# Split-weight attention with a maxout feed-forward: the lower parts of a chunk's weights made in its own period

## The chip, the cores and the metric

The kernel runs on one core of one Trainium2 chip. The metric is the device time of one execution in microseconds, as a median of several. A profile of one execution shows, for each engine, every instruction with its start, its length and the source line that issued it. The engines are TensorE (PE in the profile; its weight loads PEld), VectorE (DVE), ScalarE (ACT), GpSimd (POOL) and SyncE, whose queue of transfers is SP.

## The reference

Attention with normalized queries and keys runs on 8 batches of 12 heads, 448 rows of 64 numbers each. Its output, 3584 rows of 768, goes through a feed-forward layer with three input matrices, whose products are combined by their maximum, and one output matrix.

```python
def rmsnorm(x, g):
    rms = np.sqrt(np.mean(x * x, axis=-1, keepdims=True) + 1e-06)
    return x / rms * g
q_n, k_n = (rmsnorm(q, g_q), rmsnorm(k, g_k))
scores = scale * np.matmul(q_n, k_n.transpose(0, 1, 3, 2))
scores = scores - np.max(scores, axis=-1, keepdims=True)
attn = np.exp(scores)
attn = attn / (np.sum(attn, axis=-1, keepdims=True) + 1e-09)
attn_out = np.matmul(attn, v)
...
h = np.maximum(np.maximum(x @ w1, x @ w2), x @ w3)
return h @ w_out
```

## The kernel before

**Tiling.** A *group* `g` is a pair of heads of one batch; there are 48, six to a batch. A group is worked in four *chunks* `c` of 112 query rows, both heads side by side. `k = 4 * g + c` counts the chunks through. The first six groups (`PLAIN`) are computed in float32. From group 6 on, each float32 operand of a product is split into two float16 numbers, an upper and a lower part, and a product is the sum of three (`TERMS`: upper by upper, upper by lower, lower by upper).

**One split chunk.** `scores` (L553) puts six products into a PSUM buffer `sc`, of which there are two. `row_max` (L562, VectorE) takes the largest score of each row. `softmax` scales it (L570, ScalarE, into `nm`) and writes the exponentials of both heads over the scores in `sc` (L579, ScalarE, twice), with their sums beside them. `upper_weights` turns the sums into `rs` (L648 and L652, VectorE) and writes the upper parts of the normalized weights to `pp` (L655, ScalarE, once for each head). `lower_weights` writes the lower parts, `sc * rs` minus the upper part (L665, VectorE, once for each head); with them `sc` is read for the last time, and scores of a later chunk may go into that buffer. `turn_weights` (L675) is a DMA transpose of `pp` (three buffers) into `pt`, issued on SP. `add_values` (L703) multiplies a whole group's `pt` by the split values, and `finish` splits the result (L717 on ScalarE, then L718 on VectorE) for the feed-forward.

**The order.** All five engines run in exactly the order in which the code issues the work; each takes its own instructions from a queue and waits at the head of it. The order is made by `beat(g, i)`, called twelve times for a group. `c, part = divmod(i, 3)`: a chunk's *period* is three beats. In part 0 VectorE gets the chunk's row maximum and then the lower parts of the chunk before, and ScalarE the softmax; in part 1 come `upper_weights`; in part 2 the scores of the next chunk. Each beat also issues a piece of the feed-forward of an earlier batch on TensorE (`thirds`, L732 and L796, some two of its units a beat), and, through `later`, what these products need on VectorE and ScalarE one or more beats after (L742, L746, L752, L756, L805). Other beats square and sum the rows of a later group (`squares`, L372), split them (`upper_rows`, L434; `lower_rows`, L440), turn them on SP (`turn_rows`, L450), split the values (L525, L531), load later groups (L330, L342, L346, L347), and decode the feed-forward's weights (L188 to L205, L268 to L275, L307 to L315) during the first eleven or so groups.

In the beat, `w = g - 1` is the group whose weights are complete. Its fourth chunk is transposed at `i == 2`, the first three chunks of the group at hand at `i` = 5, 8 and 11. `add_values(w)` stands at `i == 7`.

Of the kernel before, what the change touches and what calls it, by code (L numbers as in the profile page):

```python
# [35 lines left out]
PLAIN = 6  # L36
# [3 lines left out]
def qknorm_attention_maxout_ffn_kernel(  # L40
# [48 lines left out]
    G = B * NP  # L89
# [448 lines left out]
    def scores(g, c):  # L538
        s = st[g]
        sc = ps_s.tile([P, 2, 512], F32, name="sc", tag="s")  # L540
        s["sc", c] = sc
        if g < PLAIN:
            qt = s["qs"].rearrange("p (c r) -> p c r", c=NQ)
            for h, rows in enumerate(HALVES):
                nc.tensor.matmul(
                    sc[:QP, h, :S], qt[rows, c], s["ks"][rows, KEYS[h]],
                    start=True, stop=True,
                )
            return
        qt, kt = s["qs"], s["ks"].rearrange("p a c r -> p a (c r)")  # L550
        for n, (qp, kp) in enumerate(TERMS):
            for h, rows in enumerate(HALVES):
                nc.tensor.matmul(  # L553
                    sc[:QP, h, :S], qt[rows, qp, c], kt[rows, kp, KEYS[h]],
                    start=n == 0, stop=n == len(TERMS) - 1,
                )
# [3 lines left out]
    def row_max(g, c):  # L560
        sc = st[g]["sc", c]
        nc.vector.tensor_reduce(  # L562
            sc[:QP, 0, S + 8:S + 10], sc[:QP, :, :S], axis=AX, op=ALU.max, negate=True
        )

    def softmax(g, c):
        s = st[g]
        sc = s["sc", c]
        nm = sb.tile([QP, 2], F32, name="nm", bufs=3)
        nc.scalar.activation(nm, sc[:QP, 0, S + 8:S + 10], AF.Copy, scale=down[:QP])  # L570
        if g < PLAIN:
            if c == 0:
                s["sum"] = sb.tile([QP, NQ, 2], F32, name="sum", bufs=2)
            s["e", c] = sb.tile([QP, 2, S], F32, name="e", tag="pp", bufs=3)
        for h in range(2):
            to, total = sc[:QP, h, :S], sc[:QP, 1, S + 8 + h:S + 9 + h]
            if g < PLAIN:
                to, total = s["e", c][:, h], s["sum"][:, c, h:h + 1]
            nc.scalar.activation(  # L579
                to, sc[:QP, h, :S], AF.Exp, bias=nm[:, h:h + 1], scale=down[:QP],  # L580
                accum_out=total,
            )
# [7 lines left out]
    def turn_plain(g, c):  # L590
        s = st[g]
        e = s.pop(("e", c)).rearrange("p h k -> p (h k)")
        if c == 0:
            s["pt"] = sb.tile([P, 14, S], F16, name="pt", bufs=2)
        s["turned"] = []
        sc = s.pop(("sc", c))
        for i, (u0, n) in enumerate(((0, 4), (4, 3))):
            turned = sc[:, i]
            if g < PLAIN:
                turned = ps_m.tile([P, 512], F32, name="turned", tag="m")  # L600
            for u in range(n):
                nc.tensor.transpose(
                    turned[:, u * QP:(u + 1) * QP],
                    e[:, (u0 + u) * P:(u0 + u + 1) * P], ident[:QP, :QP],
                )
            s["turned"].append((u0, n, turned))

    def keep_turned(g, c):
        s = st[g]
        for u0, n, turned in s.pop("turned"):  # L610
            nc.scalar.copy(
                pt_plain(s)[:, u0:u0 + n, c * QP:(c + 1) * QP],
                turned[:, :n * QP].rearrange("p (u q) -> p u q", u=n),
            )


    def guard_sums(g):
        rs = st[g]["sum"]
        nc.scalar.activation(rs, rs, AF.Copy, bias=SUM_EPS)

    def inverse_sums(g):
        rs = st[g]["sum"]
        nc.vector.reciprocal(rs, rs)
# [14 lines left out]
    def keep_sums(g):  # L638
        s = st[g]
        s["by"] = sb.tile([P, S], F32, name="by", tag="m", bufs=2)  # L640
        nc.scalar.copy(s["by"], s.pop("spread")[:, :S])
# [19 lines left out]
    def lower_weights(g, c):  # L661
        s = st[g]
        sc, rs, pp = s.pop(("sc", c)), s.pop(("rs", c)), s["pp", c]
        for h in range(2):
            nc.vector.scalar_tensor_tensor(  # L665
                out=pp[:, 1, h], in0=sc[:QP, h, :S], scalar=rs[:, h:h + 1],
                in1=pp[:, 0, h], op0=ALU.mult, op1=ALU.subtract,
            )
# [39 lines left out]
    def scale_plain(g):  # L708
        s = st[g]
        av = s["av"][:, :S]  # L710
        nc.vector.tensor_tensor(out=av, in0=av, in1=s.pop("by"), op=ALU.mult)
# [209 lines left out]

    def beat(g, i):
        w, n = g - 1, g + 2
        c, part = divmod(i, 3)
        k = 4 * g + c
        early = k + 1 <= 4 * PLAIN
        if part == 0:  # L930
            if g < G:
                if k > 4 * PLAIN:
                    row_max(g, c)
                softmax(g, c)
            if early:
                scores(*divmod(k + 1, 4))
            if 0 < k <= 4 * PLAIN:
                turn_plain(*divmod(k - 1, 4))
            elif 0 < k <= 4 * G:
                lower_weights(*divmod(k - 1, 4))  # L940
        if part == 1:
            if 0 < k <= 4 * PLAIN:
                keep_turned(*divmod(k - 1, 4))
            if PLAIN <= g < G:
                upper_weights(g, c)
        if part == 2:
            if early:
                row_max(*divmod(k + 1, 4))
            elif k + 1 < 4 * G:
                scores(*divmod(k + 1, 4))  # L950
        if 0 <= w < PLAIN:
            if i == 1:
                guard_sums(w)
            if i == 2:
                inverse_sums(w)
            if i == 5:
                spread_sums(w)
            if i == 6:
                keep_sums(w)
            if i == (8 if w < PLAIN else 9):  # L960
                scale_plain(w)
        if w >= 0 and i == (4 if w < PLAIN else 7):
            add_values(w)
        thirds(THIRDS[i] + (len(queue) > 1 and i % 6 == 4))
        if w >= 0 and i == (9 if w < PLAIN else 10):
            finish(w, x_of[w // NP])
        if w >= 0 and g % NP == 0 and i == (6 if w < PLAIN else 10):
            queue.append(ffn(w // NP, x_of[w // NP]))

        if g + 1 < G:  # L970
            if g + 1 < PLAIN:
                if i in (1, 4):
                    turn_whole(g + 1, "kq"[i // 4])
                if i in (2, 5):
                    keep_whole(g + 1, "kq"[i // 5])
            else:
                if i in (0, 1):
                    upper_rows(g + 1, "kq"[i])
                if i in (2, 3):
                    lower_rows(g + 1, "kq"[i - 2])  # L980
                if i in (4, 5):
                    turn_rows(g + 1, "kq"[i - 4])

        if n < G:
            if i in (0, 3):
                squares(n, "kq"[i // 3])
            if i in (2, 5):
                sum_squares(n, "kq"[i // 3])
            if i in (5, 7):
                inv_rms(n, "kq"[i // 7])  # L990
            if i == 8:
                scale_k(n)
            if i == 9:
                scale_q(n)

        if g == 0 and i < 7:
            load_v(i)
            later(3, lambda: largest_v(i))
        if 0 < g < G - 6 and i == 5:
            load_v(g + 6)  # L1000
            later(4, lambda: largest_v(g + 6))
        if g == 0 and i == 9:
            bound_v(0)
        if g > 1 and g % NP == 0 and g < G and i == 1:
            bound_v(g // NP)
        if PLAIN <= g < G and i == 9:
            scale_v(g)
        if PLAIN <= g < G and i == 11:
            upper_v(g)
        if PLAIN <= w and i == 0:  # L1010
            lower_v(w)

        if g + 3 < G:
            if i == 0:
                load_k(g + 3)
            if i == 1:
                load_q(g + 3)
        if i == 2 and w >= PLAIN:
            turn_weights(w, 3)
        if PLAIN <= g < G and i in (5, 8, 11):  # L1020
            turn_weights(g, i // 3 - 1)
        n_in = min(decoded[0], NFT * NJ)
        due_at = BLOCK_BEATS[0] * n_in + BLOCK_BEATS[1] * (decoded[0] - n_in)
        if decoded[0] < len(blocks) and clock[0] > due_at:
            later(0, lambda n=decoded[0]: prep_block(n), True)
            decoded[0] += 1
        tick()
# [41 lines left out]
```

## Time and profile before

| | before |
|---|---|
| median of 3 runs | 1101.73 us (1098.24 to 1102.97) |
| the profiled execution | 1103.44 us, its span 1101.6 us |
| PE busy | 1018.6 us (92%) |
| DVE busy | 757.8 us (69%) |
| ACT busy | 772.1 us (70%) |
| POOL busy | 702.4 us (64%) |
| mean granted PE clock | 0.957 |

The span is the time from the first to the last instruction of the profiled execution. A group's row gives the line, engine and operation, what it writes and reads, its count, then busy time and the mean length of one, then the idle time of its engine just before it and what ended that. A row of waits tells who waited for whom, for how long in total, how often, and the longest. In rows in order of time, two or more instructions of one kind that follow each other are one row, with their count behind an x.

### The profile page before, as it was taken

The numbers are of one execution on the slowest core, as the hardware profiler recorded it, in microseconds if no ns is written. First come the engines' busy times: TensorE is split into PE (matmuls) and PEld (weight loads), VectorE is DVE, ScalarE is ACT, GpSimd is POOL, SyncE is SP. The second block draws the span as 40 slices with busy tenths as digits, with TensorE's granted clock in tenths as the row PEclk, the third lists the DMA queues.
The fourth block names the chain that finished last, engine by engine and source line by source line (L and its number), as shares of the span: only waits on it lengthen the run. The fifth ranks groups of instructions, "written<-read, shape, count | busy, mean of one in ns | idle before, by whom it ended". The sixth has DMA issues, their size and how long they took to land. (4 is left out here: it accounts for less than half of the span.)

```text
span 1101.6 us, 18390 instructions
## 1 busy us (share of the span) xinstructions
PE 1018.6 (92%) x6168; PEld 501.9 (46%) x6168; DVE 757.8 (69%) x1390; ACT 772.1 (70%) x1767; POOL 702.4 (64%) x805
## 2 busy tenths in 40 slices
PE   4678768988999999999999999999999999999998
PEld 2334333434444455444544454444444454445555
DVE  3899988888667676677677776777677766762210
ACT  4599887767868678687877777778777787773001
POOL 5477988856767767678677686776867677610000
PEclk9687868998989999999999999999999999999999
DMA  5554466856787679877888789787877798563002
GB/s 149 165 164 152 129 180 137 179 115 125 151 166 149 134 151 172 160 148 133 176 155 149 136 169 175 141 151 150 170 146 143 145 166 153 106 106 73 1 1 58
DMA packets 426654, 152.29 MB, mean 138 GB/s; under 512 B 372928, under 2 KB 422336, under 8 KB 426560
## 3 DMA queue, kind: packets, MB, share of 16 engines
q1 hardware_dynamic: 425888, 150.75, 66.8%
q8 instruction: 48, 0.79, 0.3%
q10 hardware_dynamic: 672, 0.38, 0.1%
q14 instruction: 46, 0.38, 0.1%
HBM read 51.97 MB, written 11.01 MB: 57 GB/s over the span
## 5 line engine op out<-in xcount | busy, mean ns | idle before, releaser
L732 PE MATMUL acc<-xt,w_sb 128*128 128x448 f16 x2592 | 520.6, 356 | 0.6 <-ACT m L742 0.6
L732 PEld LDWEIGHTS <-w_sb 128*128 128x128 f16 x2592 | 245.1, 99 | 262.9 <-issue 53.1
L562 DVE TENSOR_REDUCE sc<-sc 112x2 f32<-112x896 f32 x192 | 209.7, 1092 | 47.8 <-PE sc L553 46.6
L579 ACT ACTIVATE sc<-sc,nm,down 112x448 f32<-112x448 f32 x336 | 234.2, 697 | 11.2
L655 ACT ACTIVATE pp<-sc,rs 112x448 f16<-112x448 f32 x336 | 194.8, 632 | 48.5 <-ACT sc L579 40.4
L665 DVE SCALAR_TENSOR_TENSOR pp<-sc,rs,pp 112x448 f16<-112x448 f32 x336 | 212.9, 675 | 3.4 <-ACT pp L655 2.9
L387 POOL TENSOR_TENSOR ri<-ri,half_neg 128x7 f32<-128x7 f32 x96 | 154.2, 1606 | 8.0
L553 PE MATMUL sc<-kt,qt 64*112 64x448 f16 x1008 | 133.7, 371 | 27.1 <-DVE pp L665 23.6
L570 ACT ACTIVATE nm<-sc,down 112x2 f32<-112x2 f32 x192 | 50.7, 264 | 149.5 <-DVE sc L562 148.2
L796 PE MATMUL acc<-wo_sb,ht 128*128 128x384 f16 x864 | 151.4, 330 | 1.4 <-DVE ht L756 0.8
L761 POOL COPY hx<-ht 128x128 f16<-128x128 f16 x48 | 15.5, 323 | 197.7 <-DVE ht L756 191.7
L796 PEld LDWEIGHTS <-ht 128*128 128x128 f16 x864 | 82.0, 99 | 67.5 <-issue 14.5
L703 PE MATMUL av<-pt,vp 128*64 128x448 f16 x1008 | 108.3, 356 | 0.0
L553 PEld LDWEIGHTS <-qt 64*112 64x112 f16 x1008 | 55.0, 128 | 96.9 <-issue 56.4
L648 DVE TENSOR_SCALAR rs<-sc 112x2 f32<-112x2 f32 x168 | 26.6, 158 | 94.7 <-ACT sc L579 94.7
L440 POOL TENSOR_TENSOR kp<-kn,kp 128x512 f16<-128x512 f32 x42 | 50.0, 1190 | 58.9 <-ACT kp L434 58.9
L703 PEld LDWEIGHTS <-vp 128*64 128x64 f16 x1008 | 49.6, 108 | 56.0 <-issue 30.4
L718 DVE SCALAR_TENSOR_TENSOR xt<-av,xt 128x448 f16<-128x448 f32 x42 | 26.2, 625 | 71.1 <-ACT xt L717 71.1
L372 DVE TENSOR_REDUCE ss<-sq 128x7 f32<-128x448 f32 x96 | 60.9, 635 | 10.6 <-ACT sq L363 6.6
L531 POOL TENSOR_TENSOR vp<-vr,vp 128x448 f16<-128x448 f32 x42 | 43.8, 1044 | 32.2 <-ACT vp L525 32.1
L440 POOL TENSOR_TENSOR qp<-qn,qp 112x512 f16<-112x512 f32 x42 | 49.3, 1173 | 21.0 <-ACT qp L434 20.8
L517 POOL TENSOR_SCALAR vr<-vr,v_up 128x448 f32<-128x448 f32 x42 | 60.7, 1446 | 0.0
(112 smaller groups left out, 1203.1 us busy)
## 6 DMA issues: line engine op xcount, KB each, us to landing
raw<-in_moe_w_dram SPq DMA_DIRECT2D x18, 768.0 KB, 4.4
qr<-in_q_dram SPq DMA_DIRECT2D x48, 224.0 KB, 3.0
vr<-in_v_dram SPq DMA_DIRECT2D x96, 96.0 KB, 2.5
kr<-in_k_dram SPq DMA_DIRECT2D x95, 96.0 KB, 3.0
raw<-in_moe_w_out_dram SPq DMA_DIRECT2D x6, 768.0 KB, 5.1
pt<-pp SPq DMA_TRANSPOSE x168, 4.1
out_dram<-osb SPq DMA_DIRECT2D x8, 336.0 KB, 3.2
out_dram<-osb SPq DMA_DIRECT2D x8, 288.0 KB, 3.7
```

Of the source, the lines that this page charges most:

```text
L372: nc.vector.tensor_reduce(sums[g % 2][:sq.shape[0], KQ[what]], sq, axis=AX, op=ALU.add)
L387: nc.gpsimd.tensor_tensor(out=ri, in0=ri, in1=half_neg[:, at], op=ALU.pow)
L440: nc.gpsimd.tensor_tensor(out=parts[:, 1], in0=n, in1=parts[:, 0], op=ALU.subtract)
L517: nc.gpsimd.tensor_scalar(out=vr, in0=vr, scalar1=v_up[:, g // NP:g // NP + 1], scalar2=None, op0=ALU.mult,)
L553: nc.tensor.matmul(sc[:QP, h, :S], qt[rows, qp, c], kt[rows, kp, KEYS[h]], start=n == 0, stop=n == len(TERMS) - 1,)
L562: nc.vector.tensor_reduce(sc[:QP, 0, S + 8:S + 10], sc[:QP, :, :S], axis=AX, op=ALU.max, negate=True)
L579: nc.scalar.activation(to, sc[:QP, h, :S], AF.Exp, bias=nm[:, h:h + 1], scale=down[:QP], accum_out=total,)
L655: nc.scalar.activation(pp[:, 0, h], sc[:QP, h, :S], AF.Copy, scale=rs[:, h:h + 1])
L665: nc.vector.scalar_tensor_tensor(out=pp[:, 1, h], in0=sc[:QP, h, :S], scalar=rs[:, h:h + 1], in1=pp[:, 0, h], op0=ALU.mult, op1=ALU.subtract,)
L703: nc.tensor.matmul(av[half, :S], vp[rows, group, vpart], pt[rows, 7 * wp + group], start=u == 0 and n == 0, stop=u == 3 and n == len(TERMS ...
L732: nc.tensor.matmul(acc[:, :S], wt[:, wp, c], xs[c][:, xp], start=(c == 0 and n == 0), stop=(c == NCT - 1 and n == 2),)
L796: nc.tensor.matmul(acc[:, :HW], lhs, wo_sb[:, f, wp, half * HW:(half + 1) * HW], start=(f == 0 and n == 0), stop=(f == NFT - 1 and n == 2),)
```

## The change

`lower_weights` of a chunk is issued in part 2 of the chunk's own period instead of part 0 of the next one, and the transposes of `pp` one beat sooner:

```diff
@@ def beat(g, i):
         if part == 0:
             if g < G:
                 if k > 4 * PLAIN:
                     row_max(g, c)
                 softmax(g, c)
...
             if 0 < k <= 4 * PLAIN:
                 turn_plain(*divmod(k - 1, 4))
-            elif 0 < k <= 4 * G:
-                lower_weights(*divmod(k - 1, 4))
...
         if part == 2:
+            if PLAIN <= g < G:
+                lower_weights(g, c)
             if early:
                 row_max(*divmod(k + 1, 4))
...
-        if i == 2 and w >= PLAIN:
+        if i == 1 and w >= PLAIN:
             turn_weights(w, 3)
-        if PLAIN <= g < G and i in (5, 8, 11):
+        if PLAIN <= g < G and i in (4, 7, 10):
             turn_weights(g, i // 3 - 1)
```

The instructions of PE, ACT and POOL stand in the same order as before. Those of DVE and SP do not. VectorE, in the middle of the program, from one row maximum over the next; before:

```order
L562 TENSOR_REDUCE sc<-sc 112x2
L665 SCALAR_TENSOR_TENSOR pp<-sc,rs,pp 112x448 x2
L648 TENSOR_SCALAR rs<-sc 112x2
L652 RECIPROCAL rs<-rs 112x2
L756 SCALAR_TENSOR_TENSOR ht<-acc,ht 128x448
L372 TENSOR_REDUCE ss_87<-sq 112x8
L562 TENSOR_REDUCE sc<-sc 112x2
```

and now, the same stretch:

```order
L562 TENSOR_REDUCE sc<-sc 112x2
L648 TENSOR_SCALAR rs<-sc 112x2
L652 RECIPROCAL rs<-rs 112x2
L756 SCALAR_TENSOR_TENSOR ht<-acc,ht 128x448
L665 SCALAR_TENSOR_TENSOR pp<-sc,rs,pp 112x448 x2
L372 TENSOR_REDUCE ss_87<-sq 112x8
L562 TENSOR_REDUCE sc<-sc 112x2
```

The pair L665 behind the first row maximum belonged to the chunk before it; the pair now in front of the second row maximum belongs to the same chunk as the sums (L648) above it. What the third beat issues besides (here L372) stands between the pair and the next row maximum.

A group's fourth chunk on VectorE, where `finish` (L718) and the feed-forward's maxima (L746) come in, from its row maximum to that of the next group's first chunk; before:

```order
L562 TENSOR_REDUCE sc<-sc 112x2
L665 SCALAR_TENSOR_TENSOR pp<-sc,rs,pp 112x448 x2
L170 TENSOR_REDUCE v_rows<-vr 128x1
L746 TENSOR_TENSOR m<-acc,m 128x448
L648 TENSOR_SCALAR rs<-sc 112x2
L652 RECIPROCAL rs<-rs 112x2
L718 SCALAR_TENSOR_TENSOR xt<-av,xt 128x448
L562 TENSOR_REDUCE sc<-sc 112x2
```

and now:

```order
L562 TENSOR_REDUCE sc<-sc 112x2
L170 TENSOR_REDUCE v_rows<-vr 128x1
L746 TENSOR_TENSOR m<-acc,m 128x448
L648 TENSOR_SCALAR rs<-sc 112x2
L652 RECIPROCAL rs<-rs 112x2
L665 SCALAR_TENSOR_TENSOR pp<-sc,rs,pp 112x448 x2
L718 SCALAR_TENSOR_TENSOR xt<-av,xt 128x448
L562 TENSOR_REDUCE sc<-sc 112x2
```

Here L170 and L746 stay between the row maximum and the sums. The pair in front of them, the third chunk's, is gone from there; the fourth chunk's pair stands behind the sums, with L718 between it and the next row maximum.

On SP, around the transposes of a group's split rows (`kt`, `qt`); before:

```order
L450 DMA_TRANSPOSE kt<-kp 128x8x128
L450 DMA_TRANSPOSE qt<-qp 128x8x112
L342 DMA vr<-in_v_dram 128x192 x2
L346 DMA vr<-in_v_dram 64x64
L347 DMA vr<-in_v_dram 64x64
L675 DMA_TRANSPOSE pt<-pp 128x14x112 x3
```

and now:

```order
L450 DMA_TRANSPOSE kt<-kp 128x8x128
L675 DMA_TRANSPOSE pt<-pp 128x14x112
L450 DMA_TRANSPOSE qt<-qp 128x8x112
L342 DMA vr<-in_v_dram 128x192 x2
L346 DMA vr<-in_v_dram 64x64
L347 DMA vr<-in_v_dram 64x64
L675 DMA_TRANSPOSE pt<-pp 128x14x112 x2
```

The transpose of the group's first chunk moved in front of the transpose of `qt` and of the loads of `vr`.

## The prediction

> **What bounds the kernel now.** I read first the busy times by stretch, cut where a new stage of the attention begins: the plain chunks, the first 24 split chunks (weights are still decoded beside them), the other 143, and the end. Columns: stretch, its length, busy time of PE, PEld, DVE, ACT and POOL with instructions in brackets, granted clock, DMA share, GB/s. The two rows below the "..." are the same view for the row maximum (L562) alone.
>
> ```profile
> 0.00:143.20 143.20, 96.52 (x497) 49.58 (x497) 116.86 (x160) 107.50 (x240) 98.40 (x102) 0.81 0.52 153
> 143.20:289.90 146.70, 126.09 (x710) 59.75 (x711) 123.23 (x216) 111.92 (x240) 112.19 (x113) 0.88 0.68 146
> 289.90:991.50 701.60, 690.61 (x4364) 335.44 (x4363) 500.02 (x985) 533.59 (x1251) 488.78 (x584) 1.00 0.79 150
> 991.50:1101.60 110.10, 105.34 (x602) 57.18 (x600) 17.67 (x31) 19.06 (x37) 3.05 (x8) 1.00 0.13 33
> ...
> 143.20:289.90 146.70, 26.12 (x24) 0.88 0.68 146
> 289.90:991.50 701.60, 156.27 (x143) 1.00 0.79 150
> ```
>
> From 289.9 us on, TensorE is busy 690.6 of 701.6 us: it is the bound. With 143 row maxima there, a chunk takes 701.6/143 = **4.91 us**, of which TensorE works 690.6/143 = 4.83. VectorE (3.5 us a chunk) and ScalarE (3.7) have room as sums; whether they have room as a chain is the question. In the stretch before, 24 chunks take 146.7/24 = 6.11 us each, with VectorE busy 123 of 146.7.
>
> Then the waits (who waited for whom, us in total, times, longest):
>
> ```profile
> ACT nm L570 <- DVE sc L562: 148.2, 139, 5.0
> DVE sc L562 <- PE sc L553: 46.6, 36, 2.2
> PE sc L553 <- DVE pp L665: 23.6, 22, 3.9
> ```
>
> The last row is the wait that this change can take away: the scores of the next chunk need the buffer that the lower parts (L665) of the last one give back. It is 23.6 us in all, 2% of the span.
>
> Then one chunk in order of time (start, length, engine, line), where nothing but its own chain holds it up:
>
> ```profile
> 991.58 1.10 DVE L562 TENSOR_REDUCE sc<-sc 112x2 f32<-112x896 f32 x1 [1.93 <-PE sc L553]
> 992.58 1.27 DVE L665 SCALAR_TENSOR_TENSOR pp<-sc,rs,pp 112x448 f16<-112x448 f32 x2
> 992.71 0.26 ACT L570 ACTIVATE nm<-sc,down 112x2 f32<-112x2 f32 x1 [2.11 <-DVE sc L562]
> ...
> 993.77 0.62 DVE L746 TENSOR_TENSOR acc<-acc,m 128x448 f32<-128x448 f32 x1
> ...
> 994.59 0.16 DVE L648 TENSOR_SCALAR rs<-sc 112x2 f32<-112x2 f32 x1 [0.20 <-ACT sc L579]
> 994.78 0.17 DVE L652 RECIPROCAL rs<-rs 112x2 f32<-112x2 f32 x1
> 995.03 1.16 ACT L655 ACTIVATE pp<-sc,rs 112x448 f16<-112x448 f32 x2 [0.48 <-ACT sc L579]
> 996.08 0.54 ACT L717 ACTIVATE xt<-av 128x448 f16<-128x448 f32 x1
> ...
> 996.66 0.62 DVE L718 SCALAR_TENSOR_TENSOR xt<-av,xt 128x448 f16<-128x448 f32 x1 [1.71 <-ACT xt L717]
> 997.20 0.62 DVE L756 SCALAR_TENSOR_TENSOR ht<-acc,ht 128x448 f16<-128x448 f32 x1
> 997.73 1.27 DVE L665 SCALAR_TENSOR_TENSOR pp<-sc,rs,pp 112x448 f16<-112x448 f32 x2
> ```
>
> The L665 pair at 992.58 belongs to the chunk before; it runs under the exponentials of this one, and costs the chain nothing. That cover is what the change gives up.
>
> **The change, part by part.** It adds and removes no instruction. ScalarE, TensorE and GpSimd keep their order; VectorE and the SP queue change theirs.
>
> *The lower parts.* Before, VectorE had the next row maximum in front of the lower parts of a chunk; now it has the lower parts in front. They need that chunk's upper parts (L655), which need its sums, its exponentials and its own row maximum. So row maximum, exponentials, upper parts, lower parts and the next row maximum become one closed chain, walked once a chunk. First, do the lower parts wait for both halves of L655, or start after one? The trace has one place where they were the waiting side:
>
> ```profile
> 531.03 1.18 ACT L655 ACTIVATE pp<-sc,rs 112x448 f16<-112x448 f32 x2
> 532.24 1.28 DVE L665 SCALAR_TENSOR_TENSOR pp<-sc,rs,pp 112x448 f16<-112x448 f32 x2 [0.59 <-ACT pp L655]
> ```
>
> They start 0.03 us after the second half ends (532.21). So, from start to start, by the rows above:
> - row maximum to nm: 992.71 - 991.58 = 1.13
> - nm and both exponentials to the sums: 994.59 - 992.71 = 1.88
> - sums and reciprocal to the upper parts: 995.03 - 994.59 = 0.44
> - both upper parts and the hand-over: 1.16 + 0.03 = 1.19
> - lower parts to the next VectorE instruction: 993.77 - 992.58 = 1.19
>
> That is **5.83 us**, already 0.92 over the 4.91 of today, with nothing else on the two engines.
>
> What else stands on that chain is read from the changed order. Over one batch of 24 chunks in the middle, VectorE has 28 long instructions between the lower parts and the next row maximum (12 L372, 6 L718, 7 L746, 3 L756), and ScalarE 16 between the second exponential and the upper parts (6 L434, 4 L805, 3 L742, 3 L752). The means of these, in the stretch from 289.9 to 991.5 us (count, busy, mean ns):
>
> ```profile
> L372 DVE TENSOR_REDUCE ss<-sq 128x7 f32<-128x448 f32 x68 | 43.2, 636 | 0.1
> L718 DVE SCALAR_TENSOR_TENSOR xt<-av,xt 128x448 f16<-128x448 f32 x36 | 22.5, 625 | 55.2 <-ACT xt L717 55.2
> L746 DVE TENSOR_TENSOR acc<-acc,m 128x448 f32<-128x448 f32 x35 | 21.8, 623 | 0.3
> L756 DVE SCALAR_TENSOR_TENSOR ht<-acc,ht 128x448 f16<-128x448 f32 x35 | 21.8, 621 | 9.8 <-ACT ht L752 8.2
> L434 ACT CAST kp<-kn 128x512 f16<-128x512 f32 x35 | 21.6, 617 | 0.0
> L805 ACT ACTIVATE osb<-acc,o_scale 128x384 f32<-128x384 f32 x33 | 18.8, 588 | 0.0
> ```
>
> One after another they overlap a little (L718 to L756 above: 0.54 us from start to start, L756 to L665: 0.53). VectorE's 28 cost 28 x 0.54 / 24 = 0.63 us a chunk. ScalarE has 0.48 us free in front of the upper parts, so a single instruction of about 0.6 costs some 0.1 and a second one its full length: I take 0.1 a chunk. VectorE work that stands behind the row maximum, or between the sums and the lower parts, lies under the exponentials or the upper parts and costs nothing; if that cover went, an L746 would add its 0.54.
>
> Sum: 5.83 + 0.63 + 0.10 = **6.56 us** a chunk against 4.91, over 143 chunks 143 x 6.56 - 701.6 = **+236 us**. TensorE's 4.83 fits under it.
>
> In the first 24 split chunks the same chain holds, with weight decoding on it:
>
> ```profile
> L200 DVE SCALAR_TENSOR_TENSOR wo_sb<-raw,wo_sb 128x768 uint32<-128x768 uint32 x6 | 8.1, 1355 | 0.1
> L205 DVE SCALAR_TENSOR_TENSOR wo_sb<-raw,wo_sb 128x768 uint32<-128x768 uint32 x6 | 6.4, 1063 | 0.0
> L268 ACT ACTIVATE w_sb<-w_sb,w_up 128x768 f32<-128x768 f32 x7 | 6.6, 949 | 0.0
> ```
>
> Of these and the like, 11 instructions of 0.9 to 2.5 us and some 33 short ones stand between lower parts and row maximum (estimate 30 us, 1.25 a chunk), and ScalarE's 27 in front of the upper parts add about 0.4 after their free 0.48. With 0.15 for crowding elsewhere: 5.83 + 1.25 + 0.4 + 0.15 = 7.63, times 24 = 183 against 146.7, **+36 us**. From 6.9 (no decoding delay on ScalarE, half of it on VectorE) to 8.2.
>
> *The scores' buffer.* The scores now find their buffer free a beat sooner; the 23.6 us of that wait go, but TensorE, no longer the bound, only idles elsewhere: nothing gained. At the end TensorE is about one chunk further ahead, so the last 110 us shorten by 0 to 6.6; I take **-3**.
>
> *The transposes* (L675) move one beat forward on SP, past the qt transpose and the vr loads. On SP they waited for the lower parts:
>
> ```profile
> SPq L675 <- DVE pp L665: 145.7, 88, 4.7
> ```
>
> Those are ready sooner by more than the beat. Behind the waiting transpose stand qt and the loads of vr. qt is read seven beats later, over two chunks or 13 us, so it hides an extra wait of even the longest 4.7; without that cover it would be 42 groups by up to 4.7, 197 us. I take 0.
>
> *The clock.* TensorE will idle about 6.56 - 4.83 = 1.7 us a chunk. What such gaps do shows in four stretches of about one clock period (columns as above):
>
> ```profile
> 58.20:61.60 3.40, 1.65 (x12) 0.86 (x9) 3.33 (x7) 2.41 (x6) 1.88 (x2) 0.99 0.32 100
> 61.60:65.00 3.40, 3.17 (x11) 1.45 (x11) 3.37 (x6) 3.25 (x10) 0.00 (x0) 0.50 0.93 276
> 242.50:245.90 3.40, 2.37 (x13) 0.98 (x12) 2.87 (x6) 2.78 (x6) 0.68 (x2) 1.00 0.60 127
> 245.90:249.30 3.40, 3.40 (x21) 1.66 (x20) 2.63 (x8) 3.04 (x8) 2.15 (x3) 1.00 0.42 106
> ```
>
> After 1.65 busy of 3.40 the clock was halved for a stretch, after 2.37 it was not. So some gaps will halve it. Each such stretch does 1.7 us of matmul work less, about a chunk's idle time, and once TensorE is full again the clock comes back: it eats the slack and adds 0 in the likeliest case. The Trainium skill, "TensorE: Matmul & The Clock Gate", part 1, gives the throttle only after an idle window of about 3.4 us; by that rule no gap here would halve the clock, and the sum stays as it is. The rows speak against it: the stretch at 58.2 was half busy and the next one ran at 0.50.
>
> Total: 1101.6 + 236 + 36 - 3 = 1371 us of span. The profiled execution took 1103.44 with its 1.8 us around the span, 1.7 above the median 1101.73, so the two offsets cancel: **1371 us** against the median.
>
> **Rivals.**
> 1. *TensorE stays the bound, at a lower clock.* If gaps halve the clock so often that the granted mean falls to 0.69 (the first stretches show 0.81 and 0.88), its 4.83 become 7.0 us a chunk: 0.44 x 143 = 63 more, 1434. For it: the rows on the clock. Against: a full TensorE gets its clock back, and below 0.74 it is full. Chance 0.10.
> 2. *The chain is shorter than I add it up:* lower parts of one head begin under the upper parts of the other, saving 0.58 a chunk, 167 x 0.58 = 97 less: 1274. The pair at 532.24 speaks against it. 0.05.
> 3. *Faster.* The wait for the scores' buffer goes and the chain stays under TensorE: 1101.7 - 23.6 = 1078. It decides at a chain of 4.91 us; the rows give 5.83. It needs 0.9 us of the chain under something that I don't see. 0.02. About 1102, the same rival half done: 0.01.
>
> **How the numbers follow.** Forecast 0.82, at 1371. Its own bounds: the VectorE work on the chain half hidden (-45) and 6.9 in the early chunks (-17) give about 1309; 8.2 there and 0.2 more of stalls a chunk (14 + 29) give 1414. With the clock rival the range is 1310 to 1440, leaving out rivals 2 and 3 and a little of the forecast. A difference of 0.5% is about what a measurement of this kernel can tell from none: faster 0.02, same 0.01, slower 0.97.
>
> **What would show it.** Right: L562 to L562 near 6.5 us from 330 to 1200 us; TensorE busy about 75 to 80% there with pieces of clock below 1; ScalarE's wait for L562 (nm) near 2 us a chunk or more; TensorE waiting for L665 or for buffers that ScalarE and VectorE hold; L665 waiting for L655 in nearly every chunk, against five times before. Wrong: L665 starting before the second L655 ends; a chunk at 5 us; or TensorE still busy over 95%, at a lower clock (rival 1).

## The result, and the profile after

The changed kernel takes **1364.55 us** (median of 4 runs, 1363.46 to 1365.44) against 1100.72 of the kernel before on the same chip: a ratio of 1.241, 95% interval 1.2379 to 1.244. The profiled execution has a span of 1361.7 us. The busy times of VectorE, ScalarE and GpSimd are those of before within half a per cent (761.3, 773.1 and 703.6 us); what was added on these three is waiting.

The stretches of the profile after, cut at the same row maxima as before (row maximum 25, 49 and 192; columns: stretch, its length, busy time of PE, PEld, DVE, ACT, POOL with instructions in brackets, granted clock, DMA share, GB/s):

```profile
0.00:140.60 140.60, 92.59 (x497) 47.32 (x497) 114.90 (x160) 107.67 (x240) 99.94 (x102) 0.87 0.53 155
140.60:317.90 177.30, 133.90 (x718) 61.58 (x719) 123.16 (x218) 111.96 (x240) 111.86 (x113) 0.87 0.59 123
317.90:1248.00 930.10, 749.45 (x4385) 350.82 (x4383) 506.64 (x984) 534.29 (x1251) 488.73 (x584) 0.94 0.58 113
1248.00:1361.70 113.70, 103.38 (x570) 55.32 (x570) 16.57 (x31) 19.15 (x37) 3.04 (x8) 0.95 0.12 32
```

and the same view for the row maximum (L562) alone, in the third of them:

```profile
317.90:1248.00 930.10, 155.82 (x143) 0.94 0.58 113
```

A chunk in the long stretch takes 930.1/143 = 6.50 us instead of 4.91, and TensorE, busy 98% there before, is busy 749/930 = 81%. The waits turned round (who waited for whom, us in total, times, longest):

```profile
ACT nm L570 <- DVE sc L562: 418.6, 172, 5.0
DVE rs L648 <- ACT sc L579: 276.2, 165, 1.9
DVE pp L665 <- ACT pp L655: 182.5, 155, 2.7
PE sc L553 <- DVE pp L665: 73.2, 63, 4.4
```

ScalarE waits for the row maximum 2.4 us a time. VectorE waits for ScalarE's upper parts in front of L665 155 times; before it was five. Its 46.6 us of waiting for scores are gone from the list: TensorE is ahead, and itself waits for the scores' buffer more than before, not less.

One chunk in order of time (start, length, engine, line); of VectorE and ScalarE only the rows of the chain, other rows are left out at each "...":

```profile
702.87 1.09 DVE L562 TENSOR_REDUCE sc<-sc 112x2 f32<-112x896 f32 x1
...
704.00 0.26 ACT L570 ACTIVATE nm<-sc,down 112x2 f32<-112x2 f32 x1 [2.35 <-DVE sc L562]
...
705.87 0.16 DVE L648 TENSOR_SCALAR rs<-sc 112x2 f32<-112x2 f32 x1 [1.40 <-ACT sc L579]
...
706.32 1.16 ACT L655 ACTIVATE pp<-sc,rs 112x448 f16<-112x448 f32 x2
...
707.50 1.28 DVE L665 SCALAR_TENSOR_TENSOR pp<-sc,rs,pp 112x448 f16<-112x448 f32 x2 [1.27 <-ACT pp L655]
...
708.70 0.61 DVE L718 SCALAR_TENSOR_TENSOR xt<-av,xt 128x448 f16<-128x448 f32 x1
...
709.23 1.09 DVE L562 TENSOR_REDUCE sc<-sc 112x2 f32<-112x896 f32 x1
```

From start to start the links are 1.13, 1.87, 0.45, 1.18 and 1.20 us, then 0.53 for the L718 that stands in between: 6.36 us from one row maximum to the next. No link of this chunk has slack: each row starts as the one above it lets it. The same links, counted from the rows in order of time of all 143 chunks, have means of 1.12, 1.88, 0.50 and 1.19 us, and 1.81 from the lower parts to the next row maximum: 6.50 in all. The first, second and fourth stay within 0.04 us of their values here in every chunk.

### The profile page after: what moved, and what is told of

The parts are those of the page before. It is cut to its first block, busy times and chain, and to the rows that moved or that the text cites. A ratio compares the mean times of both kernels' runs of the same rounds, so it can differ in the third digit from the quotient of the medians.

```text
span 1361.7 us, 18413 instructions
## 1 busy us (share of the span) xinstructions
PE 1079.3 (79%) x6168; PEld 515.0 (38%) x6168; DVE 761.3 (56%) x1390; ACT 773.1 (57%) x1767; POOL 703.6 (52%) x805
## 5 line engine op out<-in xcount | busy, mean ns | idle before, releaser
L732 PE MATMUL acc<-xt,w_sb 128*128 128x448 f16 x2592 | 552.2, 369 | 55.1 <-DVE ht L756 31.0
L732 PEld LDWEIGHTS <-w_sb 128*128 128x128 f16 x2592 | 251.9, 101 | 343.2 <-issue 147.9
L665 DVE SCALAR_TENSOR_TENSOR pp<-sc,rs,pp 112x448 f16<-112x448 f32 x336 | 214.3, 679 | 190.2 <-ACT pp L655 182.5
L553 PE MATMUL sc<-kt,qt 64*112 64x448 f16 x1008 | 140.3, 385 | 128.8 <-DVE pp L665 73.2
L562 DVE TENSOR_REDUCE sc<-sc 112x2 f32<-112x896 f32 x192 | 209.2, 1089 | 0.7 <-PE sc L545 0.6
L796 PE MATMUL acc<-wo_sb,ht 128*128 128x384 f16 x864 | 169.6, 352 | 40.4 <-ACT ht L752 21.8
L648 DVE TENSOR_SCALAR rs<-sc 112x2 f32<-112x2 f32 x168 | 26.8, 160 | 276.2 <-ACT sc L579 276.2
L553 PEld LDWEIGHTS <-qt 64*112 64x112 f16 x1008 | 58.9, 132 | 206.5 <-issue 113.9
L796 PEld LDWEIGHTS <-ht 128*128 128x128 f16 x864 | 85.6, 104 | 119.2 <-issue 45.8
L383 POOL TENSOR_SCALAR ri<-ss 128x7 f32<-128x7 f32 x96 | 25.7, 267 | 156.7 <-DVE ss L372 156.7
L372 DVE TENSOR_REDUCE ss<-sq 128x7 f32<-128x448 f32 x96 | 61.3, 640 | 10.3 <-ACT sq L363 6.3
```

The source lines that it names most:

```text
L372: nc.vector.tensor_reduce(sums[g % 2][:sq.shape[0], KQ[what]], sq, axis=AX, op=ALU.add)
L553: nc.tensor.matmul(sc[:QP, h, :S], qt[rows, qp, c], kt[rows, kp, KEYS[h]], start=n == 0, stop=n == len(TERMS) - 1,)
L562: nc.vector.tensor_reduce(sc[:QP, 0, S + 8:S + 10], sc[:QP, :, :S], axis=AX, op=ALU.max, negate=True)
L665: nc.vector.scalar_tensor_tensor(out=pp[:, 1, h], in0=sc[:QP, h, :S], scalar=rs[:, h:h + 1], in1=pp[:, 0, h], op0=ALU.mult, op1=ALU.subtract,)
L732: nc.tensor.matmul(acc[:, :S], wt[:, wp, c], xs[c][:, xp], start=(c == 0 and n == 0), stop=(c == NCT - 1 and n == 2),)
L796: nc.tensor.matmul(acc[:, :HW], lhs, wo_sb[:, f, wp, half * HW:(half + 1) * HW], start=(f == 0 and n == 0), stop=(f == NFT - 1 and n == 2),)
```

## The experiments

Each was compared with runs of the kernel before on the same chip. The lengths of a chunk are those of the 143 chunks from row maximum 49 to 192 in each profile.

**1. The two halves of the change apart.** `turn_only` is the kernel before with the transposes alone a beat sooner; `lower_only` has the lower parts alone in their own period:

```diff
@@ turn_only, against before
-        if i == 2 and w >= PLAIN:
+        if i == 1 and w >= PLAIN:
             turn_weights(w, 3)
-        if PLAIN <= g < G and i in (5, 8, 11):
+        if PLAIN <= g < G and i in (4, 7, 10):
@@ lower_only, against after
-        if i == 1 and w >= PLAIN:
+        if i == 2 and w >= PLAIN:
             turn_weights(w, 3)
-        if PLAIN <= g < G and i in (4, 7, 10):
+        if PLAIN <= g < G and i in (5, 8, 11):
```

> The kernel before with the second half of the change alone: the transposes of pp one beat sooner, the lower parts where they were. The closed chain (theory): VectorE's order is that of before, no chain; a chunk stays at 4.91 us and the time at 1101, within 5 us. The rival that the transposes' new place on SP costs the time: near 1364.

> The first half of the change alone: the lower parts in the third beat of their own period, the transposes at the beats of before. Theory: 1364 within 5 us, 6.50 us a chunk. The rival of the transposes: near 1101; if both halves share the cost, between.

`turn_only` takes 1099.34 us, a ratio of 1.001 (0.9998 to 1.0022); `lower_only` takes 1364.43, a ratio of 1.2427 (1.2408 to 1.2447). The place of the lower parts makes the whole difference, and that of the transposes none that can be measured, in the old order of VectorE (`turn_only` against the kernel before) or in the new one (`lower_only` against the changed kernel's 1364.55).

**2. One L665 out of the chain.** In `one_head` head 0's lower parts stay in front of the next row maximum; head 1's go behind it, where both were before (`lower_weights` gets the heads as a third argument; that part of the edit is left out here):

```diff
@@ one_head, against after: def beat(g, i), part 0
                 turn_plain(*divmod(k - 1, 4))
+            elif 0 < k <= 4 * G:
+                lower_weights(*divmod(k - 1, 4), (1,))
...
             if PLAIN <= g < G:
-                lower_weights(g, c)
+                lower_weights(g, c, (0,))
```

> The changed kernel, with the lower parts of one head in front of the next row maximum and those of the other head behind it. Theory: one of the two L665 leaves the chain, 1.19 / 2 = 0.60 us a chunk, 167 x 0.60 = 100 us: 1264 within 10, some 5.9 us a chunk. The rival that TensorE's lowered clock sets the time: its work is the same, so near 1364. If the cost were the wait for the upper parts alone, whatever stands behind it: near 1364 too.

It takes 1265.95 us, a ratio of 1.1532 (1.1514 to 1.1549). The row maximum in its long stretch:

```profile
306.70:1152.10 845.40, 155.80 (x143) 0.97 0.66 125
```

845.4/143 = 5.91 us a chunk, 0.59 less than 6.50. The L665 that remains still waits for the upper parts (188.9 us, 160 times), and yet the time is 98 us below that of `lower_only` and of the changed kernel. So that wait alone isn't the cost; the length of what stands between the upper parts and the next row maximum counts too.

**3. Other work out of the chain.** In `sums_later` the sums of squares of the split groups go from the third beat to the one after it, behind the row maximum:

```diff
@@ sums_later, against after: def beat(g, i)
-            if i in (2, 5):
-                sum_squares(n, "kq"[i // 3])
+            at = (3, 6) if g >= PLAIN else (2, 5)
+            if i in at:
+                sum_squares(n, "kq"[at.index(i)])
```

> The changed kernel, with the sums of squares (L372) of the split groups issued one beat later, so that they stand behind the row maximum and not between the lower parts and it. Theory: 12 L372 of 24 chunks leave the chain, 0.54 us each, 0.27 a chunk, 167 x 0.27 = 45 us: 1319 within 12. If only the five links of a chunk's own chain count, or TensorE bounds: 1364.

It takes 1319.31 us, a ratio of 1.2016 (1.1998 to 1.2034). A chunk takes 892.0/143 = 6.24 us, 0.27 less, by this row:

```profile
313.40:1205.40 892.00, 155.86 (x143) 0.94 0.62 118
```

The same 12 instructions in 24 chunks cost 45 us more over the whole program in the one place than in the other, which is all of their 0.54 us each.

**4. Is it TensorE after all?** Both kernels, with the third of the three products of each sum left out in the first layer (lower part of the weights by upper part of the input):

```diff
@@ def layer1
-            for n, (wp, xp) in enumerate(TERMS):
+            for n, (wp, xp) in enumerate(TERMS[:2]):
```

> The changed kernel, whose first feed-forward layer leaves out the third product of each sum (lower by upper): 864 of 2592 products L732 less, some 310 us of TensorE's work. Theory: the chain of VectorE and ScalarE sets the time, so the split chunks stay at 6.50 us and only the end, where TensorE works alone, shortens by a third of its 61 us of L732: 1364 - 20 = 1344, within 8. The rival that TensorE at a lower clock sets the time: about 1364 - 310 = 1054 to 1100.

> The kernel before with the same third products left out. Theory: there TensorE is the bound, so this time the cut counts, until the chain of before (row maximum, exponentials, upper parts, without the lower parts) or the other engines bound: 4.1 to 4.4 us a chunk instead of 4.91, and 20 us less at the end: 960 to 1010. If the chain of VectorE and ScalarE already bound the kernel before: near 1080.

`after_two_terms` takes 1344.45 us, a ratio of 1.2238 (1.2214 to 1.2263) to the whole kernel before. In the long stretch:

```profile
319.20:1249.70 930.50, 672.65 (x3727) 298.27 (x3726) 506.29 (x985) 534.95 (x1251) 489.30 (x584) 0.88 0.57 113
```

It has 658 of 4385 matmuls less, and the stretch is 930.5 us long instead of 930.1: there TensorE sets nothing. The clock fell further, from 0.94 to 0.88, and that changed nothing either. The 20 us came at the end, as expected: the last stretch is 92.2 us (1249.7 to 1341.9) instead of 113.7.

`before_two_terms` takes 1055.2 us, a ratio of 0.9605 (0.9586 to 0.9625): there the cut counts, so TensorE was a bound. But it counted less than expected: 960 to 1010 us was missed. The chunk stops at 678.3/143 = 4.74 us, not at 4.1 to 4.4. The row maximum in its long stretch, and TensorE's wait for the scores' buffer:

```profile
284.50:962.80 678.30, 155.93 (x143) 0.97 0.82 155
```

```profile
PE sc L553 <- DVE pp L665: 97.4, 61, 4.2
```

It grew from 23.6 to 97.4 us. TensorE is busy 589.6 us of the long stretch, so it is idle for 88.7, and this wait is 72.9 of that; in the kernel before it is 7.4 in its long stretch. With less work for TensorE, a second bound at about 4.74 us a chunk thus shows, and mostly in this wait. That it stands so close behind TensorE's 4.83 in the kernel before too is an inference, and what sets it isn't shown here.

**5. The lower parts sooner, but behind the next row maximum.** `max_first` issues the next chunk's scores, its row maximum and then the lower parts in the third beat:

```diff
@@ max_first, against after: def beat(g, i), part 0
-                if k > 4 * PLAIN:
-                    row_max(g, c)
                 softmax(g, c)
...
@@ part 2
-            if PLAIN <= g < G:
-                lower_weights(g, c)
             if early:
                 row_max(*divmod(k + 1, 4))
             elif k + 1 < 4 * G:
                 scores(*divmod(k + 1, 4))
+                row_max(*divmod(k + 1, 4))
+            if PLAIN <= g < G:
+                lower_weights(g, c)
```

`max_first_old_turn` is the same with the transposes at their old beats, and `max_first_two_terms` the same with the cut of experiment 4.

> The changed kernel, with the next row maximum issued in the third beat too, behind the next scores and in front of the lower parts. Theory: the lower parts of a chunk lie under the next exponentials again and the chain is open; TensorE bounds at 4.91 us: 1090 to 1108. A better time than before would come from row maxima that no longer stand behind L372 and L746. If the early place of the lower parts itself were the cost: near 1364.

> The kernel with the next row maximum and then the lower parts in the third beat, but the transposes of pp at the beats of before. If the 5 us that it gained over the kernel before come from the new places of the row maximum and the lower parts: 1094, within 2. If the sooner transposes have a part in it: between 1094 and 1099.

> The same order of row maximum and lower parts with the sooner transposes, and the first layer without its third products (lower by upper), as in the two kernels with less of TensorE's work. If the kernel before with that cut stood at 1055 because its scores waited for L665, that wait is shorter here and the time falls clearly below, 1000 to 1040. If ScalarE's and VectorE's own queues held it there: 1045 to 1055.

`max_first` takes 1093.83 us, a ratio of 0.9953 (0.9939 to 0.9967): the change's loss is gone, and it is a little faster than the kernel before. `max_first_old_turn` takes 1093.59, a ratio of 0.9962 (0.9948 to 0.9976), the same within the intervals: the transposes have no part in it that can be measured. In the profile of `max_first`, the two stretches of split chunks:

```profile
143.10:286.40 143.30, 122.30 (x704) 57.61 (x705) 121.90 (x215) 110.34 (x239) 108.38 (x112) 0.91 0.72 148
286.40:982.50 696.10, 689.50 (x4371) 334.13 (x4370) 498.99 (x983) 532.69 (x1253) 488.88 (x585) 1.00 0.80 152
```

and its waits:

```profile
PE sc L553 <- DVE pp L665: 10.7, 6, 3.6
DVE sc L562 <- PE sc L553: 170.6, 140, 2.8
```

The early stretch is 143.3 us instead of 146.7, the long one 696.1 instead of 701.6, with TensorE busy 99% of it. VectorE now waits for the scores nearly every time, as it should under a bound by TensorE, and TensorE's wait for L665 fell from 23.6 to 10.7 us. Which of the two, the sooner row maximum or the shorter wait, gave the 5 us was not tested. (The two profiled executions lie 8 us apart, the medians 5.)

`max_first_two_terms` takes 1033.27 us, a ratio of 0.9405 (0.9389 to 0.9422). It lies in the range that was expected if the scores' wait for L665 held that kernel, but the wait is only halved:

```profile
PE sc L553 <- DVE pp L665: 44.9, 33, 3.4
```

```profile
285.60:940.90 655.30, 585.77 (x3722) 275.31 (x3720) 501.90 (x983) 528.25 (x1253) 489.52 (x586) 0.98 0.84 161
```

A chunk stops at 655.3/143 = 4.58 us, with no engine full. What holds it there was not tried and stays open.

## Why the prediction was right, step by step

| stretch | predicted | measured |
|---|---|---|
| plain chunks | 0 | 143.2 to 140.6: -2.6 |
| first 24 split chunks | +36 | 146.7 to 177.3: +30.6 |
| the other 143 | +236 | 701.6 to 930.1: +228.5 |
| the end | -3 | 110.1 to 113.7: +3.6 |
| sum | +269, 1371 us | +260.1, span 1361.7 |

The two stretches of split chunks were forecast 13 us too long, and the end 7 us too short; that these offset each other in part is luck, and small beside the +260.

- **The closed chain.** Right. Its five links were to take 5.83 us; in the chunk shown they take 1.13 + 1.87 + 0.45 + 1.18 + 1.20 = 5.83. Experiments 2 and 3 show both kinds of terms by themselves: one L665 of 0.60 measured 0.59 a chunk, twelve L372 in 24 chunks, 0.27, measured 0.27. The whole chunk came to 6.50 against 6.56. By the means over all chunks, the other work of VectorE on the chain came to 1.81 - 1.19 = 0.62 us a chunk (0.63 in the sum), and that of ScalarE to 0.50 - 0.44 = 0.06 (0.10 in the sum). So the chunk was right because each term was, and not because errors cancelled. TensorE's 81% lies just over the 75 to 80% that were named.
- **The first 24 chunks.** Right in kind, 0.24 us a chunk too long (177.3/24 = 7.39 against 7.63), since the delays of the weight decoding were an estimate. The same count of links over these 24 chunks gives 1.15 us of other work of VectorE (1.25 in the sum), 0.28 of ScalarE (0.4) and 0.13 of other delays (0.15): each was a little too large, ScalarE's most.
- **The scores' buffer.** That the removed wait brings nothing was right. That it goes was wrong: TensorE now arrives earlier and waits longer at the same place, 73.2 us instead of 23.6.
- **The end.** Wrong in sign. The prediction let TensorE carry its lead of about a chunk into the end. It has the lead, and can't use it:

```profile
1253.05 0.55 ACT L752 ACTIVATE ht<-acc 128x448 f16<-128x448 f32 x1
1253.47 0.58 ACT L525 CAST vp<-vr 128x448 f16<-128x448 f32 x1
1253.65 0.13 PEld L796 LDWEIGHTS <-ht 128*128 128x128 f16 x2 [6.67 <-ACT ht L752]
1253.65 0.82 PE L796 MATMUL acc<-wo_sb,ht 128*128 128x384 f16 x2 [6.29 <-ACT ht L752]
...
1254.49 0.61 DVE L756 SCALAR_TENSOR_TENSOR ht<-acc,ht 128x448 f16<-128x448 f32 x1
1255.16 0.13 PEld L796 LDWEIGHTS <-ht 128*128 128x128 f16 x2 [1.37 <-DVE ht L756]
1255.16 11.35 PE L796 MATMUL acc<-wo_sb,ht 128*128 128x384 f16 x52 [0.68 <-DVE ht L756]
```

  The next product needs the last hidden tile, whose split (L752, L756) stands in ScalarE's and VectorE's queues behind the last chunk's own chain. TensorE, which has done sooner what it could do, idles 6.29 us for it, where it idled 0.60 in the profile before. From the last row maximum to the end of that split VectorE needs about 0.7 us more, since the pair L665 now stands in front of L718 and L756. And TensorE starts again at a lower clock (0.50 granted from 1253.6 to 1260.4 us): the next 52 matmuls take 11.35 us, where the same 52 took 8.62 in the last chain of the profile before. The two, 0.7 and 2.7 us, make up most of the 3.6.
- **The transposes.** Right at 0 (experiment 1). But the lower parts were to be ready sooner by more than the beat, and SP waits for them longer, not less: 145.7 us before, and after:

```profile
SPq L675 <- DVE pp L665: 290.9, 116, 6.4
```

  This costs no time that shows: the links of the chain add up to the whole 6.50 us without it.
- **The plain chunks** were not to change, and their order doesn't. In `max_first`, where it doesn't either, they end at 143.1 us. In the profiles of all experiments, whose plain chunks are the same, they end between 140.6 and 143.7: executions differ by this much.
- **Rival 1**, TensorE bounding at a lower clock: refuted by experiment 4. The clock did fall, to a mean of 0.94 and not to the 0.69 of this rival, and its cost stayed under TensorE's idle time. **Rival 2**, the heads overlapping: refuted; L665 at 707.50 starts 0.02 us after the second upper part ends (706.32 + 1.16), and in all 143 chunks it starts 1.18 to 1.22 us after the first one starts. **Rival 3**, faster: refuted by the result; a chain below 4.91 us was what it needed.

## What to carry to other kernels

In a queue that runs in order, put in front of an instruction only what doesn't depend on that instruction's own last round: as soon as it does, two engines' work becomes one closed chain, and its links add up once a round, whatever the engines' busy shares say. Count the chain from start to start in the trace and compare it with the time that the bound engine takes for a round; here 5.83 against 4.91 us decided it before any further detail. And weigh a wait that could be removed against the cover that is given up for it. Here the wait was 23.6 us in the whole program, 7.4 of it in the long stretch; the cover given up was 1.19 us under the exponentials in every round, and in about half of the rounds also the row maximum under the upper parts.

## What the runs showed that was not expected

That gaps in TensorE's work would halve its clock was forecast; that a single one of 2.15 us is enough, and what the lower clock costs, are new. In the profile after, around one gap of 2.15 us (TensorE in order of time):

```profile
699.80 1.11 PE L732 MATMUL acc<-xt,w_sb 128*128 128x448 f16 x5
703.06 0.77 PE L553 MATMUL sc<-kt,qt 64*112 64x448 f16 x6 [2.15 <-issue]
```

and the busy times of four stretches of 3.4 us there, the granted clock third from the end:

```profile
697.60:701.00 3.40, 3.31 (x18) 1.50 (x16) 1.35 (x4) 2.75 (x7) 1.00 (x1) 1.00 0.53 100
701.00:704.40 3.40, 1.34 (x10) 0.73 (x11) 2.85 (x5) 1.02 (x4) 2.97 (x7) 0.99 0.08 16
704.40:707.80 3.40, 3.40 (x11) 1.40 (x10) 0.70 (x4) 3.35 (x9) 3.38 (x3) 0.50 1.16 163
707.80:711.20 3.40, 3.40 (x22) 1.53 (x21) 3.04 (x5) 1.37 (x4) 1.03 (x1) 1.00 0.69 133
```

The gap lies in the second stretch. In the third the clock is half, though TensorE is busy in all of it, and in the fourth it is full again. Over the long stretch the lower clock costs TensorE 749.5 - 690.6 = 59 us of busy time for nearly the same products (4385 and 4364 matmuls in the traces), all of it under idle time by experiment 4. The Trainium skill, "TensorE: Matmul & The Clock Gate", part 1, gives the lower clock as the default and after at least one idle window of about 3.4 us; here a gap of 2.15 us was enough.
